# Two attentions, one gate: whole-tile stores of q and k, and row maxima on neighbouring partitions

## The chip, the cores and the metric

The kernel runs on one core of a Trainium2 chip. The metric is the device time of one execution in microseconds (us). TensorE (PE) multiplies, with its weight loads (PEld) beside it; VectorE (DVE), ScalarE (ACT) and GpSimd (POOL) do the rest; SyncE (SP) issues every transfer (DMA).

## The reference

There are 2048 positions of width 640 and 32 heads of 20. Branch A cuts the positions into four segments of 512: causal softmax attention inside a segment, plus a read from a memory matrix that earlier segments filled. Branch B is causal attention in a sliding window of 256. A gate mixes them.

```python
# A, for segment s of 4, head by head (L = 512, Dh = 20)
p = softmax(qs @ ks.T * scale + causal);  a_dot = p @ vs
a_mem = (phi(qs) @ M) / (phi(qs) @ z + 1e-6)          # phi(t) = t + 1 if t > 0 else exp(t)
o = g_h * a_mem + (1 - g_h) * a_dot
M += phi(ks).T @ vs;  z += phi(ks).sum(0)
a = concat(o) @ wo
# B, all 2048 positions
p = softmax(where(0 <= i - j < 256, q @ k.T * scale, -1e9));  b = (p @ v) @ wo_b
g = sigmoid((x * gate_w).sum(-1));  out = g * a + (1 - g) * b
```

## The kernel before

**The work.** `T` counts 16 pieces: four segments times four head groups (g = 0 and 1 are the halves of branch A's heads, 2 and 3 those of B). A piece projects q and k in five tiles of 128 rows by 512 positions (`gemm2`, L578), in split precision: x and the weights are each a rounded half and a residual (`split_h` L516, `split_l` L532), and three products make one. It projects v (`v_mm`, L730), and then has four units `u` (64 in all) of four heads each.

**Stacks.** A projected tile is itself split into a rounded half and a residual, `ml` (`m_high` on ACT, L599; `m_low` on DVE, L603), and stored to an image in DRAM (`qk_store`, L633 and L635: one of the two writes half and residual, the other the half once more). `stack_read` (L804, L807, L809) loads from it a stack `qks` of 128 partitions: two halves of 64, for two heads each, with 60 rows of q and the matching rows of k. One matmul over 60 rows thus gives a product of two split numbers. Before, a tile's rows ran over the borders of the image's blocks of 160 rows, so that a tile was stored in one or two pieces of 32 to 128 rows (`runs_of`), each with two transfers.

**Maxima.** `max_mm` (L833) computes all logits once, `max_red` (L843, DVE) takes each query's maximum; the 16 columns of maxima are split into half and residual (`max_high`, `max_low`), turned (`max_turn`), stored to DRAM (`max_store`, L859) and loaded back as two more rows of q in each half of the stack, partitions 60 and 61 and 124 and 125, by two transfers (`max_rows`, L863). The rows of k there hold -1 (`init_pad`, L485), so that the score matmul over 62 rows (`st_mm`, L887) subtracts the maximum. ACT takes the exponential (`st_exp`, L894), POOL cuts the triangle (`select`, L900 and L903), TensorE multiplies with v in four column groups (`av_mm`, L919).

**Memory.** phi(q) and phi(k) (L640 to L648) are stored by `phi_store` (L657); `mem_load` (L927) brings phi(k) into `pks`, `mem_query` (L933) phi(q) into `qfs`; `mem_add` (L966) and `mem_read` (L946) use them. `o_store` (L1035) keeps the results for the last product (`gemm2` again with `ohl`, and `gemm`, L570, for the last tile).

**The order** is written out by a planner in the program. Each step is added with a due time, an engine, an estimated cost, the buffers that it makes, changes and reads, and, for a transfer, its size. `order` then simulates the engines and picks, for each, the step that could start first, ties going to the smaller rank: the due time plus a shift by kind and a nudge, both from tables.

```python
rank = items[i][19] + nudge[i].get(step, 0.0)
...
most = min(some)[0] + (TP if pe else TO)
pick = min((z for z in some if z[0] <= most), key=lambda z: z[1:])
```

The matmuls on 64 rows belong to one of two half arrays, `pe0` and `pe1`, and two of them run side by side. A product that changes halves in its middle has a `join` there (L593), an empty instruction of ACT or DVE that waits for the first half. Steps on SP are issued in the order that the planner wrote, one behind the other; `ml` and `phi` have two buffers each, the stacks four, the ring `xst` of loads of x and of results four.

Of the kernel before, what the change touches and what calls it, by code (L numbers as in the profile page):

```python
# [10 lines left out]
F32 = mybir.dt.float32  # L11
# [22 lines left out]
WIN = 256  # L34
KW = WIN + L
# [82 lines left out]
class Plan:  # L118
# [56 lines left out]
    def link(self):  # L175
# [8 lines left out]
        for i, (t, _, eng, dur, fn, a, new, mod, put, get, size, pace, cols, _, bank, _, _, mark, behind, _) in enumerate(items):  # L184
# [217 lines left out]
def attention(ctx, tc, const, dram, xt, wqk, wv, wo, beta, o_dram, out):  # L402
# [79 lines left out]
    def init_pad(d, row, off):  # L482

        n = 32 * row // 128
        nc.sync.dma_start(bass.AP(tensor=d.tensor, offset=d.offset + off, ap=[[n, 128], [1, n]]), B["neg"][:, 0:n])  # L485
# [845 lines left out]
```

## Time and profile before

| | |
|---|---|
| time, median of 3 runs | 988.43 us (988.43, 983.97, 991.27) |
| profiled execution | 980.1 us, its span 978.4 us |
| TensorE clock granted | 1.000 |
| busy PE, PEld, DVE | 967.9, 812.6, 761.4 us |
| busy ACT, POOL | 651.7, 637.2 us |
| moved by DMA | 248.56 MB, mean 254 GB/s |

The profile is one execution. A line such as "L578 PE MATMUL ... x2400 | 453.5, 398 | 3.6" names a line of the program, an engine and an operation, what it writes and reads, how many there are; then the busy time of the group in us, the mean of one in ns, and the idle time of the engine just before them. Busy times of groups that run side by side overlap. The chain is the work that ended last, followed back from the end: a line there carries the share of the time in which that work was what all else waited for. In the view by stretches, each engine has its busy time in us with its number of instructions, then come the granted clock, the share of the DMA engines and GB/s. In the view of one line, DMA_DIRECT2D durations are the time that SP took to issue, as least/median/most in ns.

### The profile page before, as it was taken

Reading aid. Unit: us, or ns where it says so; the run is one execution under the profiler, and the core shown is the slowest. Engines: PE = TensorE matmul, PEld = TensorE weight load, DVE = VectorE, ACT = ScalarE, POOL = GpSimd, SP = SyncE. Lnnn points to the kernel's source line nnn. Section 1 sums busy time; section 2 is a strip of 40 time slices with the busy share of each in tenths; the row PEclk is TensorE's granted clock in tenths of the full one; section 3 lists DMA queues with packets and bytes.
Section 4 is the critical chain, followed back from the end, with each engine's and each line's share of the span. In section 5 each row is a group of like instructions: output and inputs, shape, how many; then the busy total and the mean of one; then the engine's idle time right before and its main releaser. Section 6 shows DMA issues by size and latency. Waiting matters only on the chain.

```text
span 978.4 us, 30482 instructions
## 1 busy us (share of the span) xinstructions
PE 967.9 (99%) x11295; PEld 812.6 (83%) x11295; DVE 761.4 (78%) x2626; ACT 651.7 (67%) x1432; POOL 637.2 (65%) x864
## 2 busy tenths in 40 slices
PE   8999999999999999999999999999999999999998
PEld 6997798888878888879888798888988888887776
DVE  3269789898899876988868888698767886788944
ACT  4527767877686776675876676676676676765671
POOL 5424467847666696757966479595795676956850
PEclk9999999999999999999999999999999999999999
DMA  8998989798898879699887887979867798487533
GB/s 276 306 306 267 290 277 275 252 293 265 279 260 283 277 220 308 205 314 298 260 264 242 254 280 207 311 224 333 285 230 234 222 296 270 137 268 215 180 99 103
DMA packets 158036, 248.56 MB, mean 254 GB/s; under 512 B 52032, under 2 KB 68288, under 8 KB 157888
## 3 DMA queue, kind: packets, MB, share of 16 engines
q1 hardware_dynamic: 157888, 246.62, 79.7%
q8 instruction: 89, 1.46, 0.6%
q14 instruction: 59, 0.48, 0.1%
HBM read 150.88 MB, written 95.68 MB: 252 GB/s over the span
## 4 chain that ended last, share of the span: by engine, by line
PE 92%; DVE 3%; DMA 3%; ACT 0%; issue 0%; POOL 0%; SPq 0%; DVEq 0%
PE bank L578 43%; PE bank L919 15%; PE bank L730 14%; PE bank L833 9%; PE bank L887 8%; DVE bank L843 2%; PE bank L570 2%; DMA wst<-wqk 1%; PE bank L946 1%; PE bank L966 1%; DMA wvs<-wv 1%; DMA xst<-xt 1%; DVE mx L843 0%; DVE ot L990 0%; SPq L524 0%
## 5 line engine op out<-in xcount | busy, mean ns | idle before, releaser
L894 ACT ACTIVATE P<-bank 128x512 f32<-128x512 f32 (+2 forms) x768 | 381.3, 556 | 148.2 <-PE bank L887 98.2
L578 PE MATMUL bank<-xhl,w 64*128 64x512 f32 x2400 | 453.5, 398 | 3.6 <-ACT xhl L516 2.8
L578 PEld LDWEIGHTS bank<-xhl,w 64*128 64x128 f32 x2400 | 325.4, 186 | 14.8 <-ACT xhl L516 3.7
L833 PE MATMUL bank<-qks 60*128 60x384 f32 (+3 forms) x1024 | 309.1, 334 | 1.3 <-DVE ot L990 0.8
L843 DVE CUSTOM_DVE_ANT_0 bank<-bank,mask_b 128x384 f32<-128x384 f32 (+2 forms) x512 | 259.7, 553 | 28.3 <-PE bank L833 21.1
L730 PE MATMUL bank<-wv,xhl 64*128 64x320 f32 (+1 forms) x1920 | 280.6, 313 | 0.2 <-POOL wv L532 0.2
L843 DVE CUSTOM_DVE_ANT_0 bank<-bank,mask_a 128x128 f32<-128x128 f32 (+3 forms) x512 | 239.9, 509 | 39.4 <-PE bank L833 29.2
L887 PE MATMUL bank<-qks 62*128 62x384 f32 (+3 forms) x1216 | 261.1, 301 | 0.4 <-DVE ot L990 0.2
L730 PEld LDWEIGHTS bank<-wv,xhl 64*128 64x128 f32 x1920 | 238.8, 186 | 3.2 <-issue 1.2
L578 PE MATMUL bank<-ohl,w 64*128 64x512 f32 x1050 | 226.3, 399 | 0.1
L532 POOL TENSOR_TENSOR w<-wst,w 128x640 fp32r<-128x640 f32 x112 | 174.9, 1565 | 77.9 <-ACT w L516 77.0
L900 POOL TENSOR_SCALAR_AFFINE_SELECT P<-P 128x512 f32<-128x512 f32 x256 | 161.5, 640 | 76.7 <-ACT P L894 71.6
L887 PEld LDWEIGHTS bank<-qks 62*128 62x128 f32 x1216 | 195.8, 185 | 15.3 <-issue 3.3
L833 PEld LDWEIGHTS bank<-qks 60*128 60x128 f32 x1024 | 177.5, 184 | 20.8 <-issue 6.2
L919 PE MATMUL bank<-P,vau 128*32 128x384 f32 (+3 forms) x2432 | 159.9, 407 | 0.2
L578 PEld LDWEIGHTS bank<-ohl,w 64*128 64x128 f32 x1050 | 152.9, 185 | 8.6 <-issue 3.3
L843 DVE DVE_READ_ACCUMULATOR2_ANT mx<- 128x1 f32 x1024 | 142.5, 139 | 0.0
L919 PEld LDWEIGHTS bank<-P,vau 128*32 128x32 f32 x2432 | 69.3, 110 | 78.6 <-issue 63.5
L516 ACT ACTIVATE w<-wst 128x640 fp32r<-128x640 f32 x121 | 89.4, 741 | 40.1 <-PE bank L578 15.7
L990 DVE STREAM_TRANSPOSE ot<-bank 128x512 f32<-128x512 f32 x64 | 45.8, 715 | 64.0 <-PE bank L919 61.6
L903 POOL TENSOR_SCALAR_AFFINE_SELECT P<-P 128x512 f32<-128x512 f32 x112 | 70.8, 641 | 4.5 <-ACT P L894 4.1
L532 POOL TENSOR_TENSOR wv<-wvs,wv 128x322 fp32r<-128x322 f32 x80 | 65.2, 834 | 11.8 <-ACT wv L516 11.5
(72 smaller groups left out, 758.9 us busy)
## 6 DMA issues: line engine op xcount, KB each, us to landing
qks<-dqk SPq DMA_DIRECT2D x32, 1024.0 KB
wst<-wqk SPq DMA_DIRECT2D x80, 320.0 KB
qks<-dkb SPq DMA_DIRECT2D x24, 768.0 KB
qks<-dqb SPq DMA_DIRECT2D x32, 512.0 KB
o_dram<-ot SPq DMA_DIRECT2D x64, 256.0 KB
wst<-wo SPq DMA_DIRECT2D x41, 320.0 KB
wvs<-wv SPq DMA_DIRECT2D x16, 805.0 KB
xst<-o_dram SPq DMA_DIRECT2D x35, 256.0 KB
```

The source lines that it names most:

```text
L516: nc.scalar.activation(dst, src, AF.Copy)
L532: EN[e].tensor_tensor(out=t[:, 1], in0=B.pop(src), in1=f(t[:, 0]), op=ALU.subtract)
L578: z = nc.tensor.matmul(B[key], B[wkey][64 * r:64 * r + 64, a, 128 * c:128 * c + 128], B[xkey, c][64 * r:64 * r + 64, b], start=start, stop ...
L730: z = nc.tensor.matmul(B["v", T, b][:, :n], B[("x", s), c][64 * r:64 * r + 64, a, 128 * b:128 * b + 128], B["wv", T, c][64 * r:64 * r + 64 ...
L833: nc.tensor.matmul(psum(("mx", u, p, b, r))[:, :n], fr(q), keys(u, 3 * DH, r, p, c0, n), start=True, stop=True)
L843: nc.vector.tensor_tensor_reduce(out=x, in0=x, in1=mk, scale=1.0, scalar=BIG, op0=ALU.add, op1=ALU.max, accum_out=B["M", u][:, j:j + 1])
L887: nc.tensor.matmul(B[k][:, c:c + 128 * n], keys(u, K, r, p, WIN + 128 * kb, 128), fr(q[64 * r:64 * r + K, L * p + 128 * q0:L * p + 128 * ( ...
L894: nc.scalar.activation(B["P", u, b][:, 2 * r + p, c0:c1], B["st", u, b, p, r][:, c0:c1], AF.Exp, scale=SCALE)
L900: nc.gpsimd.affine_select(out=v, in_=v, pattern=[[0, 4], [1, 128]], compare_op=ALU.is_ge, fill=0.0, base=0, channel_multiplier=-1)
L903: nc.gpsimd.affine_select(out=v, in_=v, pattern=[[0, 4], [-1, 128]], compare_op=ALU.is_gt, fill=0.0, base=0, channel_multiplier=1)
L919: nc.tensor.matmul(o[32 * j:32 * j + 32, 128 * q0:128 * (q0 + n)], v[:, VA * h:VA * h + 32], t[:, j, c:c + 128 * n], start=(b == 0 and i = ...
L990: nc.vector.transpose(t, B["o", u])
```

## The change

- **The weight columns** of q and k are laid out anew on the host, so that of a piece's five projected tiles two hold q alone (16 of the 20 columns of each head, one tile for each half of the stack), two k alone, and the middle one 64 rows of q and 64 of k.
- **Stores.** The four plain tiles go out whole, 128 rows at a time: one transfer writes the rounded half to both of its places, reading it twice, and waits for `m_high` alone; the other writes the residual. The middle tile goes out in six transfers of 64 rows. `phi_store` writes a tile in one transfer, or 64 rows of the middle one.
- **Stacks.** The image of the upper half starts at row 68 of each stack. Partitions 0 to 59 are the first half, 68 to 127 the second, 62 to 65 the four rows of maxima, and 60, 61, 66 and 67 are padding: q has zeros there and in the rows to be loaded, k has -1. One transfer a unit loads the maxima. The score matmul reads 64 rows in both halves, the maxima's matmul 60 in the lower and 64 in the upper. The columns of maxima are ordered to fit, so `max_high` and `max_low` write with a step.
- **Pads** are 8 transfers instead of 16, the zeros from `pks`.
- **Queries** of the memory come in 6 transfers instead of 8 for two units.
- **The first segment's x** is loaded into the five buffers `ys` instead of the ring `xst`.
- **The planner**: `join` is costed at 0.06 on both engines; nudges go by finer groups of steps, and their table is replaced whole.

```diff
+MAXR, R1 = 62, 68
...
+GROUPS = dict(
+    max_high='M', max_low='M', max_turn='M', max_store='N', max_rows='N', o_turn='O', den_eps='O', den_rec='O',
...
 NUDGE = dict(
-    a={22: 0.6},
-    c={12: 1, 39: 1.4, 47: 1.4, 51: -1.1, 53: 2.1, 74: 2.9},
...
+    a={49: -4.3},
+    c={30: -0.98, 35: 0.4, 74: 1.87},
...
+    def group(self, z):
+        return GROUPS.get(z[4].__name__, self.kind(z))
...
             for name in get:
+                if name[0] == "first":
+                    s = slot(name[1])
+                    deps[i].add(s["base"])
+                    s["gets"].append(i)
+                    continue
...
-        nudge = [NUDGE.get(self.kind(z), {}) for z in items]
+        nudge = [NUDGE.get(self.group(z), {}) for z in items]
...
-    def init_pad(d, row, off):
-        n = 32 * row // 128
-        nc.sync.dma_start(bass.AP(tensor=d.tensor, offset=d.offset + off, ap=[[n, 128], [1, n]]), B["neg"][:, 0:n])
+    def init_pad(d, row, off, key):
+        n = 8 * (R1 - 3 * DH) * row // 128
+        src, m = pks if key == "im" else B[key], min(n, L)
+        ap = [[n, 128], [1, n]] if n == m else [[n, 128], [m, n // m], [1, m]]
+        nc.sync.dma_start(bass.AP(tensor=d.tensor, offset=d.offset + off, ap=ap),
+                          src[:, 0:n] if n == m else src[:, 0:m].unsqueeze(1).to_broadcast([128, n // m, m]))
...
     def load(tag, pool, bufs, width, key, src):
         B[key] = (xpool.tile([128, L], F32, name=tag, tag=tag, bufs=bufs)[:, :width] if tag == "xst" else
+                  work.tile([128, L], F32, name=tag, tag=tag, bufs=bufs) if tag == "ys" else
...
-    def runs_of(m, kinds=(0, 1)):
...
+    PARTS = ((0, 0), (0, 1), None, (1, 0), (1, 1))
+    PIECES = [[(0, 128, 0), (0, 128, 1)], [(0, 128, 0), (0, 128, 1)], [(64 * w, 64, i) for i in range(3) for w in range(2)],
+              [(0, 128, 0), (0, 128, 1)], [(0, 128, 0), (0, 128, 1)]]
...
-    def qk_store(T, m, n, twice):
-        w, half, at, r, c = runs_of(m)[n]
+    def qk_store(T, m, n):
+        r, c, i = PIECES[m][n]
+        w, half = PARTS[m] or (r // 64, 0)
         d, row, off = image(T, w)
-        ml = f(B["ml", ("m", T, m)][r:r + c])
-        z = (2 - 2 * w) if twice else w
-        off += (512 * half + 8 * DH * z + at) * row
-        if twice:
-            nc.sync.dma_start(bass.AP(tensor=d.tensor, offset=off, ap=[[row, c], [1, L]]), ml[:, 0])
+        step = 8 * DH * row
+        if c == 128:
+            x = f(B["ml", ("m", T, m)])[:, i]
+            off += 8 * R1 * half * row + (2 - w) * step * i
+            if i:
+                nc.sync.dma_start(bass.AP(tensor=d.tensor, offset=off, ap=[[row, 128], [1, L]]), x)
+            else:
+                nc.sync.dma_start(bass.AP(tensor=d.tensor, offset=off, ap=[[row, 128], [(1 + w) * step, 2], [1, L]]),
+                                  bass.AP(tensor=x.tensor, offset=x.offset, ap=[list(x.ap[0]), [0, 2], [1, L]]))
         else:
-            nc.sync.dma_start(bass.AP(tensor=d.tensor, offset=off, ap=[[row, c], [8 * DH * row, 2], [1, L]]), ml)
+            x = f(B["ml", ("m", T, m)])[r:r + 64, i // 2]
+            off += 128 * row + ((0, 1 + w, 2 - w)[i]) * step
+            nc.sync.dma_start(bass.AP(tensor=d.tensor, offset=off, ap=[[row, 32], [8 * R1 * row, 2], [1, L]]), x)
...
-    def phi_store(T, m, n):
...
+    def phi_store(T, m, w):
         d = dphi[head(T)[0]]
+        off = d.offset + 2 * QB * w * L
+        if PARTS[m]:
+            nc.sync.dma_start(bass.AP(tensor=d.tensor, offset=off + PARTS[m][1] * L, ap=[[2 * L, 128], [1, L]]), B["phi", T, m])
+        else:
+            nc.sync.dma_start(bass.AP(tensor=d.tensor, offset=off + 256 * L, ap=[[L, 64], [1, L]]), B["phi", T, m][64 * w:64 * w + 64])
...
-                    add(t0 + NC * dt - 0.01, AD, (0.2, 0.08), join, k, mod=[k], off=-9)
+                    add(t0 + NC * dt - 0.01, AD, (0.06, 0.06), join, k, mod=[k], off=-9)
...
-        add(t + 1.1e-4, DVE, 0.61, m_low, k, mod=[ml], get=[k], off=EV)
+        add(t + 1.1e-4, DVE, 0.61, m_low, k, put=[ml], get=[k], off=EV)
+        for n, (r, c, i) in enumerate(PIECES[m]):
+            add(t + 3e-4, SP, 0.55, qk_store, T, m, n, put=[("dq", T)] if m or n else [],
+                new=[] if m or n else [(("dq", T % 4) if g < 2 else ("dq", T), 1, ("dq", T))],
+                get=[("first", ml) if i == 0 or c == 64 and i == 1 else ml], size=(4096 if c == 128 and i == 0 else 2048) * c, packet=2048)
...
     def max_mm(u, p, b, r):
+        K = 64 if r else 3 * DH
...
+    def mparts(u):
+        return mrs[u % 2].rearrange("p (r z j) -> p z r j", z=2, j=8)
...
-        nc.scalar.activation(mrs[u % 2][:, 0:16], B["M", u], AF.Copy)
+        nc.scalar.activation(mparts(u)[:, 0], B["M", u].rearrange("p (r j) -> p r j", j=8), AF.Copy)
...
-    def max_rows(u, r):
+    def max_rows(u):
         d = B["dmx", u]
-        nc.sync.dma_start(qks[u % NQ][64 * r + 3 * DH:64 * r + 3 * DH + 2, 0:2 * L], bass.AP(
-            tensor=d.tensor, offset=d.offset + 2 * L * r, ap=[[4 * L, 2], [1, 2 * L]]))
+        nc.sync.dma_start(qks[u % NQ][MAXR:MAXR + 4, 0:2 * L], bass.AP(tensor=d.tensor, offset=d.offset, ap=[[2 * L, 4], [1, 2 * L]]))
...
     def st_mm(u, b, p, r, i):
-        q, K = qks[u % NQ], 3 * DH + 2
+        q, K = qks[u % NQ], 64
...
-    for i, (d, row, off, k) in enumerate(pads):
-        add((-5.2, -2.5, 0, 2)[i // 4] + 0.01 * i, SP, DI, init_pad, d, row, off, get=["neg"], put=[k], size=2 ** 16 * row // L, packet=row)
+    for t, d, row, off, src, k in pads:
+        add(t, SP, DI, init_pad, d, row, off, src, get=[src], put=[k, "iz"] if src == "im" else [k], size=2 ** 17 * row // L, packet=2 * row)
...
-                plan_split(-20 + 0.02 * c, -20.01 + 0.02 * c, "xhl", xpool, NX, "xst", NXS, L, (("x", 0), c),
+                plan_split(-20 + 0.02 * c, -20.01 + 0.02 * c, "xhl", xpool, NX, "ys", NC, L, (("x", 0), c),
...
-        for r in range(2):
-            add(t + .04 + .001 * r, SP, DJ, max_rows, u, r, get=[("dmx", u)], put=[("qr", u)], size=8192, packet=4096, rings=2)
+        add(t + .04, SP, DJ, max_rows, u, get=[("dmx", u)], put=[("qr", u)], size=16384, packet=4096, rings=4)
...
-                for j in range(8 * (1 - u % 2)):
+                for j, (i, x) in enumerate(((0, 0), (1, 0), (2, 0), (3, 0), (0, 1), (1, 1)) if u % 2 == 0 else ()):
...
-                    add(u + ML + 0.001 * i, SP, 0.65, mem_load, T, g // 2, i, get=[("dphi", T, 1), "im"],
+                    add(u + ML + 0.001 * i, SP, 0.65, mem_load, T, g // 2, i, get=[("dphi", T, 1), "im", "iz"],
```

More of the change, by code (lines that the diff above doesn't have):

```diff
@@ L704, in plan_m @@
         add(t + 1e-4, ACT, 0.5, m_high, k, new=[("ml", 2, ml)], get=[k], off=EV)
-        add(t + 1.1e-4, DVE, 0.61, m_low, k, mod=[ml], get=[k], off=EV)
-        for n, z in enumerate(runs_of(m)):
-            for twice in range(2):
-                add(t + 3e-4, SP, 0.55, qk_store, T, m, n, twice, put=[("dq", T)] if m or n or twice else [],
-                    new=[] if m or n or twice else [(("dq", T % 4) if g < 2 else ("dq", T), 1, ("dq", T))],
-                    get=[ml], size=(4096, 2048)[twice] * z[4], packet=2048)
-        runs = phi_rows(T, m) if g < 2 else []
-        if runs:
-            zs = {w: min(x for x in range(NC) for y in phi_rows(T, x) if y[0] == w) for w in {z[0] for z in runs}}
-            new = [w for w in zs if zs[w] == m]
+        add(t + 1.1e-4, DVE, 0.61, m_low, k, put=[ml], get=[k], off=EV)
[3 more added lines that the diff above has]
+                get=[("first", ml) if i == 0 or c == 64 and i == 1 else ml], size=(4096 if c == 128 and i == 0 else 2048) * c, packet=2048)
+        ws = [w for w in phi_kinds(T) if not PARTS[m] or PARTS[m][0] == w] if g < 2 else []
+        if ws:
             add(t + 4e-5, ACT, 0.5, phi_neg, T, m, new=[("phi", 2, ph)], get=[k], off=EV)
@@ L717, in plan_m @@
             add(t + 6e-5, DVE, 0.61, phi_sum, T, m, get=[k], mod=[ph], off=EV)
-            for n, z in enumerate(runs):
-                w = z[0]
-                add(t + 7e-4, SP, 0.7, phi_store, T, m, n, get=[ph], size=2048 * z[4],
-                    new=[(("dphi", g, w), 1, ("dphi", T, w))] if w in new else [], put=[] if w in new else [("dphi", T, w)])
-                new = [x for x in new if x != w]
+            for w in ws:
+                add(t + 7e-4, SP, 0.6, phi_store, T, m, w, get=[ph], size=2 ** 18 if PARTS[m] else 2 ** 17,
+                    new=[(("dphi", g, w), 1, ("dphi", T, w))] if m == 2 * w else [], put=[] if m == 2 * w else [("dphi", T, w)])
     def v_mm(T, b, r, c, i, start, stop):
@@ L777, in plan_v @@
                 if n == 3 * NC - 1:
-                    add(t + n * dt / 3 + 1e-4, AD, (0.2, 0.08), join, k, mod=[k], off=-9)
+                    add(t + n * dt / 3 + 1e-4, AD, (0.06, 0.06), join, k, mod=[k], off=-9)
             plan_vout(t + 2 * NC * dt - 0.01 + j * 1e-3, T, b + j)
@@ L831, in max_mm @@
         c0, n = max_keys(u, b)
-        q = qks[u % NQ][64 * r:64 * r + 3 * DH, L * p + 128 * b:L * p + 128 * b + 128]
-        nc.tensor.matmul(psum(("mx", u, p, b, r))[:, :n], fr(q), keys(u, 3 * DH, r, p, c0, n), start=True, stop=True)
+        K = 64 if r else 3 * DH
+        q = qks[u % NQ][64 * r:64 * r + K, L * p + 128 * b:L * p + 128 * b + 128]
+        nc.tensor.matmul(psum(("mx", u, p, b, r))[:, :n], fr(q), keys(u, K, r, p, c0, n), start=True, stop=True)
     def max_red(u, p, b, r):
@@ L1126, in attention @@
     add(-14, POOL, 0.5, init_neg, new=[("ot", 2, "neg")])
[L1127 to L1130 removed]
+    pads = [(t, ds[i], row, (8 * 128 * h + 8 * 3 * DH) * row, src, ("ik", k, i)) for t, k, ds, row, h, src, i in
+            ((-5.2, 0, dqk, L, 0, "im", 0), (-5.19, 0, dqk, L, 1, "neg", 0), (-2.5, 1, dqb, L, 0, "im", 0), (-2.49, 2, dkb, S, 0, "neg", 0),
+             (-2.48, 0, dqk, L, 0, "im", 1), (-2.47, 1, dqb, L, 0, "im", 1), (0, 0, dqk, L, 1, "neg", 1), (2, 2, dkb, S, 0, "neg", 1))]
+    for t, d, row, off, src, k in pads:
+        add(t, SP, DI, init_pad, d, row, off, src, get=[src], put=[k, "iz"] if src == "im" else [k], size=2 ** 17 * row // L, packet=2 * row)
     add(-13, POOL, 2.0, c_mask, put=["mk"])
@@ L1257, in attention @@
             if s > 0:
-                for j in range(8 * (1 - u % 2)):
+                for j, (i, x) in enumerate(((0, 0), (1, 0), (2, 0), (3, 0), (0, 1), (1, 1)) if u % 2 == 0 else ()):
                     qk = ("qf", u // 2)
-                    add(u + QF + 0.001 * j, SP, DI, mem_query, T, g // 2, j % 4, j // 4, get=[("dphi", T, 0)],
-                        new=[] if j else [("qf", NF, qk)], put=[qk] if j else [], size=DH * 2048, packet=1024, rings=10, late=DS)
+                    add(u + QF + 0.001 * j, SP, DI, mem_query, T, g // 2, i, x, get=[("dphi", T, 0)],
+                        new=[] if j else [("qf", NF, qk)], put=[qk] if j else [], size=(1 + i // 2) * DH * 2048, packet=1024 * (1 + i // 2),
+                        rings=10, late=DS)
                 add(te + 0.03, DVE, 0.72, o_turn, u, 1, get=[("num", u), ("nub", u)], put=[ok])
```

92 lines of the change are left out of this document (49 added, 43 removed).

## The prediction

> **What bounds the kernel now.** I read the page's busy shares first, then the chain that ended last for the whole span and cut into stages, then TensorE's groups with their shapes kept apart, and last SyncE's own queue.
>
> ```profile
> PE 967.9 (99%) x11295; PEld 812.6 (83%) x11295; DVE 761.4 (78%) x2626; ACT 651.7 (67%) x1432; POOL 637.2 (65%) x864
> PE 92%; DVE 3%; DMA 3%; ACT 0%; issue 0%; POOL 0%; SPq 0%; DVEq 0%
> by line: PE bank L578 42.7%; PE bank L919 15.5%; PE bank L730 13.6%; PE bank L833 8.6%; PE bank L887 8.2%; DVE bank L843 2.0%; PE bank L570 1.8%; DMA wst<-wqk 1.4%; PE bank L946 1.3%; PE bank L966 0.7%; DMA wvs<-wv 0.7%; DMA xst<-xt 0.6%; D
> ```
>
> TensorE is busy 967.9 of 978.4 us and carries 92% of the chain; SyncE's queue, on which most of the change lies, carries 0%. But busy is not full: two 64-row matmuls can run side by side on the two halves of the array, and one that runs alone counts as just as busy. How full the time is comes from the instructions:
>
> ```profile
> 26.79 3.58 PE bank L578 x31
> 957.15 17.28 PE bank L570 x75
> L578 PE MATMUL bank<-xhl,w 64*128 64x512 f32 x2400 | 453.5, 398 | 3.6 <-ACT xhl L516 2.8 <-DVE xhl L532 0.5 <-DVE mx L843 0.3
> L578 PE MATMUL bank<-ohl,w 64*128 64x512 f32 x1050 | 226.3, 399 | 0.1
> L730 PE MATMUL bank<-wv,xhl 64*128 64x320 f32 x1440 | 208.0, 313 | 0.0
> L833 PE MATMUL bank<-qks 60*128 60x384 f32 x576 | 188.3, 354 | 0.3
> L887 PE MATMUL bank<-qks 62*128 62x384 f32 x384 | 122.6, 351 | 0.1
> L887 PE MATMUL bank<-qks 62*128 62x256 f32 x352 | 80.3, 287 | 0.0
> L887 PE MATMUL bank<-qks 62*128 62x128 f32 x352 | 72.9, 219 | 0.0
> L730 PE MATMUL bank<-wv,xhl 64*128 64x322 f32 x480 | 72.7, 312 | 0.2 <-POOL wv L532 0.2
> L833 PE MATMUL bank<-qks 60*128 60x512 f32 x128 | 49.6, 412 | 0.0
> L833 PE MATMUL bank<-qks 60*128 60x256 f32 x160 | 45.1, 296 | 0.0
> L887 PE MATMUL bank<-qks 62*128 62x512 f32 x128 | 44.5, 420 | 0.4 <-DVE ot L990 0.2
> L833 PE MATMUL bank<-qks 60*128 60x128 f32 x160 | 36.7, 240 | 1.0 <-DVE ot L990 0.8 <-DVE mx L843 0.2
> ```
>
> On the chain, 31 paired matmuls of 512 columns took 3.58 us, 0.1155 us each (75 whole-array ones took 17.28, 0.230 each, which is the same rate): 0.226 ns a column when both halves work. At that rate L578's 3450 need 398 us; L730's 615,360 columns 139; L833's 348,160 columns (576x384 + 128x512 + 160x256 + 160x128) 79; L887's, by the same count of columns, 79; L570 17; and L919, L946 and L966, at their 17.5% of the chain, 171. Together 883 us of the 978.4: **95 us are lost** to matmuls without a partner, to turns between the kinds, and at both ends. A change that leaves TensorE's instructions as they are can only win from these 95. Their place shows in the chain by stage, here 0 to 60, 60 to 240, 240 to 900 and 900 to 979 us:
>
> ```profile
> by line: PE bank L578 48.8%; PE bank L730 21.4%; DMA wvs<-wv 11.2%; DMA xst<-xt 10.1%; SPq L524 3.3%; POOL wv L532 1.5%; PE bank L833 1.0%; ACT wv L516 0.8%; issue 0.8%
> by line: PE bank L578 35.7%; PE bank L730 14.4%; PE bank L919 13.5%; PE bank L887 9.8%; PE bank L833 9.3%; DVE bank L843 5.7%; DMA wst<-wqk 3.3%; DVE mx L843 1.2%; PE bank L966 1.0%; POOL w L532 0.9%; issue 0.8%; DVE ot L990 0.7%; ACT phi L
> by line: PE bank L578 45.6%; PE bank L919 17.2%; PE bank L730 14.3%; PE bank L833 9.8%; PE bank L887 8.8%; PE bank L946 2.0%; DMA wst<-wqk 1.2%; PE bank L966 0.8%; ACT w L516 0.1%; DVE ot L990 0.1%; DVE bank L843 0.1%; ACT P L894 0.1%; issu
> by line: PE bank L578 30.3%; PE bank L570 21.9%; PE bank L919 16.9%; DVE bank L843 10.6%; PE bank L887 5.9%; PE bank L833 2.5%; DVE mx L843 1.8%; issue 1.5%; DVE ot L990 0.9%; DVE ot L993 0.9%; DVE ys L1070 0.9%; DVE ot L1030 0.7%; DVE den
> ```
>
> Up to 60 us two loads and what they release are on the chain (wvs 11.2% and xst 10.1%, 12.8 us). From 60 to 240 the terms shown off TensorE (DVE 7.6%, wst 3.3%, POOL 0.9%, issue 0.8%) make 12.6%, 23 us; from 240 to 900 TensorE's own lines add up to 98.5%, which leaves 1.5%, 10 us in eleven times 60. At the end it is DVE's row maxima again. So two thirds of the run has next to nothing to give.
>
> **The change part by part.** *TensorE's instructions*: the same count. The maxima of the upper half read 64 rows for 60, the scores 64 for 62. Rows cost nothing here: with 512 columns the rows above have 412 ns at 60, 420 at 62, 398 and 399 at 64. 0 us.
>
> *SyncE's queue*:
>
> ```profile
> L633 SPq DMA_DIRECT2D dqk<-ml x64: 308/516/2123, 23.8 to 814.5; - x64
> L635 SPq DMA_DIRECT2D dqk<-ml x64: 312/520/1736, 19.6 to 814.0; - x64
> L657 SPq DMA_DIRECT2D dphi<-phi x48: 527/684/1219, 39.4 to 793.9; - x48
> L863 SPq DMA_DIRECT2D qks<-dmx x128: 233/257/2676, 73.5 to 936.9; - x128
> L933 SPq DMA_DIRECT2D qfs<-dphi x96: 273/335/2375, 253.3 to 891.1; - x96
> L485 SPq DMA_DIRECT2D dqk<-ot x8: 319/430/550, 4.4 to 16.6; - x8
> ```
>
> A head group and segment (16 of them) stores q and k with 14 transfers instead of 16: 32 fewer at about 0.518, 16.6 us. Stores of phi go from 48 to 36 (8.2 us at 0.684), rows of maxima from 128 to 64 (16.4 at 0.257), queries from 96 to 72 (8.0 at 0.335), pads from 16 to 8 (3.4 at 0.430). That is 140 transfers and 53 us of issue, the bytes being the same. Directly it is worth 0, since no SPq line but L524 at the start is on the chain above; through what stands behind it in the queue it is worth something only where a load was late: wst at 3.3% of 180 us and 1.2% of 660, 14 us. TensorE had other work in most of that, as its idle there says:
>
> ```profile
> 0.00:20.00 20.00, 15.73 (x111) 10.81 (x113) 7.45 (x12) 10.05 (x19) 9.18 (x23) 1.00 0.86 271
> 60.00:120.00 60.00, 59.19 (x704) 49.84 (x701) 54.04 (x205) 40.29 (x94) 27.68 (x40) 1.00 0.90 276
> 180.00:240.00 60.00, 59.06 (x694) 48.76 (x692) 51.90 (x197) 47.13 (x111) 37.21 (x52) 1.00 0.86 275
> ```
>
> 0.94 us idle in the stretch with the late wst. Between nothing and 14 I take 2, near the idle rows. DVE, with 54.04 of 60 us from 60 to 120, is not relieved: its 512 x 2 reductions stay. So late next, where a load comes earlier, is DVE, with 5.7% of that stage.
>
> One joined load of maxima for two is counted above by its issue alone, 0.257 us, since the two loads stood one behind the other and no row gives a landing by itself. The Trainium skill (DMA: Bandwidth & Descriptors, "Latency and other measured facts") speaks against counting more: a tiny transfer has a shortest round trip, which it gives as about 800 ns, whatever its size, so that joining two saves no latency. By that rule the sum stays as it is; by full saving of a round trip in each of 64 units it would be up to 51 us more, all of it off the chain, and no run here shows it.
>
> *The start.* All five chunks of x now get buffers of their own (the ring had four):
>
> ```profile
> 4.37 3.30 SPq L485 DMA_DIRECT2D dqk<-ot  x4
> 8.12 0.33 SPq L524 DMA_DIRECT2D xst<-xt  x1
> 12.52 0.50 PE L578 MATMUL bank<-xhl,w 64*128 64x512 f32 x2 [1.62 <-ACT xhl L516]
> 9.08 6.70 DMA wvs<-wv
> ```
>
> The fifth load is issued at 8.12, behind four pads that take 3.30 us, and TensorE idles 1.62 us for it at 12.52. Issued with the other four, at about 3, it comes before it is wanted: 1.6 us. The two pads left in that place give wvs, issued at 9.08, at most half of 3.30, 1.65 us; but the transfers share engines that are 0.86 busy, so what x gains wvs may lose. I take 2 us, between 0 and 3.3.
>
> *What waits anew.* The first store of a tile waits for the rounded half alone and not for the residual (one DVE operation, 0.68 us, earlier). Both halves' scores now wait for one row load; SP issued the second 0.26 us after the first, so nothing is lost. The loads into pks also wait for the pads that read its zeros; those pads are issued in the first 20 us or so and the first such load at 59. The new maxima layout makes three small operations strided; 64 units times a few ns. Together 0.
>
> *The order.* The list of nudges is replaced whole, so every engine's order changes outside the arithmetic above. No row prices it. Its bounds: the 23 us of the stage from 60 to 240 falling to the 1.5% of the next one, minus 20; and a loss of the size that the same program shows between its runs, 983.97 to 991.27, plus 7. I take minus 1, close to nothing, as two thirds of the run is nearly full.
>
> Sum: 2 + 2 + 1 = 5 us less. The profiled execution took 980.1 us, 1.7 beyond its span, and goes to 975; the median of the runs shown is 8.3 above it, and from 988.4 the forecast is **983 us**.
>
> **The rivals.** *Faster: the freed queue reaches TensorE.* The Trainium skill (Perfetto Trace Analysis, "Identifying the Most-Contended Engine") judges TensorE's headroom by the weight loads' share, not by matmul time. By that, 83% here, there would be more room than the idle shows; the 95 us found above agree. The mechanism in this kernel: between 60 and 240 us stacks, rows and weights come earlier, scores and products find partners, and the 12.6% off TensorE fall by half, 11 us, with 2 to 3 from the start: 988.4 - 14 = 974. For it speaks that SP stands in a row there, against it that DVE and not a transfer leads that stage's waits.
>
> *No change: the start's gain is taken back.* The DMA engines are 0.86 busy in the first 20 us; an earlier fifth chunk delays wvs, on whose landing the first v products hang, and later stages hold no wait that SP ends. 988, give or take 3.
>
> *Slower: ScalarE held by the stores.* The middle tile of five holds 64 rows of q and 64 of k and now goes out in six transfers where it had four; two buffers of ml are all there are, and the rounding copy in ScalarE's order waits until they have landed:
>
> ```profile
>   DMA dqb<-ml: 7.5, 1
>   DMA dqk<-ml: 2.7, 2
> ```
>
> Behind it on ScalarE stand the exponentials (L894), which free the score banks. Two more issues of 0.52 in each of 16 groups are 16.6 us; were all of it to reach TensorE, less 2 at the start, 1003; it decides once these waits exceed some 25 us where they are 10 to 12 now. Against it: the other four tiles go out in two transfers each, and earlier.
>
> That the change doesn't do what it says can be left out: the counts of transfers follow from the loops.
>
> **How the numbers follow.** About 1% (10 us) is what a measurement of this kernel can tell from no change. Forecast, 978.5 to 986: 0.36. No change, 986 to 992: 0.20. Faster, 963 to 978.5 with 974 in its middle: 0.29. Slower, 992 to 1006: 0.15, of which 0.06 is still within 1%. So faster by over 1% has 0.29, within 1% 0.62, slower by over 1% 0.09. The range of 8 in 10 takes in the bounds of the start and the queue and leaves out the far ends of the two outer cases, about 0.1 each: 968 to 998.
>
> **What would show it.** Right: SyncE's counts as above; the fifth xst issued before 5 us and no idle of 1.6 us at 12; TensorE's busy time 960 to 965 with the same counts; the chain from 240 us still over 97% TensorE. Wrong: waits of the ml copies on their own stores over 25 us (the slower rival); the non-TensorE share from 60 to 240 under 7% (the faster one); or from 240 us on a share off TensorE of 4% and more, which would mean that the new order, and no transfer, sets the time.

## The result, and the profile after

The changed kernel takes **975.38 us** (median of 6 runs, 974.45 to 977.93) against 987.22 for the kernel before (6 runs, 983.77 to 991.27): ratio 0.9885, 95% interval 0.9855 to 0.9915, or 11.8 us less. Measured again, the same pair gave 0.9925 (0.9897 to 0.9952). That lies in the range of the rival "faster" and below the forecast's own 978.5 to 986.

The two profiled executions, of 980.1 and 976.76 us, are only 3.4 us apart by their spans (978.4 and 975.0). The one of before stood at the fast end of its kernel's runs, the one of after inside its narrow band. The page of after, its busy line and the engines of the chain:

```profile
PE 965.6 (99%) x11295; PEld 809.5 (83%) x11295; DVE 765.7 (79%) x2624; ACT 649.9 (67%) x1435; POOL 636.3 (65%) x863
PE 88%; DMA 5%; POOL 3%; DVE 2%; issue 1%; ACT 1%; SPq 0%; POOLq 0%; DVEq 0%; ACTq 0%
```

TensorE does as many instructions in 2.3 us less, and SyncE's queue is still at 0% of the chain. The chain by stage, 0 to 60, 60 to 240 and 240 to 900 us:

```profile
by line: PE bank L605 42.1%; PE bank L754 23.9%; DMA wst<-wqk 10.4%; DMA wvs<-wv 10.3%; SPq L551 4.2%; SPq L510 2.6%; PE bank L858 2.1%; POOL wv L559 1.5%; issue 1.0%; ACT wv L542 0.8%
by line: PE bank L605 41.8%; PE bank L754 18.3%; PE bank L947 17.1%; PE bank L858 10.8%; PE bank L915 10.4%; PE bank L998 1.3%; ACT P L922 0.3%; issue 0.0%
by line: PE bank L605 40.6%; PE bank L947 15.3%; PE bank L754 13.7%; PE bank L858 8.8%; PE bank L915 7.7%; PE bank L978 2.0%; DMA wst<-wqk 1.7%; issue 1.5%; DMA dphi<-phi 1.4%; DMA qks<-dmx 1.0%; POOL w L559 0.9%; PE bank L998 0.8%; DMA wvs
```

(The lines moved: L605 was L578, L754 was L730, L858 was L833, L868 was L843, L915 was L887, L922 was L894, L947 was L919.) From 60 to 240 us what is off TensorE fell from 12.6% to 0.3%. From 240 to 900 it rose from 1.5% to 6.5% in the terms shown alone; TensorE's own lines there add up to 88.9%, where they were 98.5%. The stretches say what this is worth in TensorE's time:

```profile
0.00:20.00 20.00, 17.98 (x127) 13.79 (x128) 7.72 (x14) 10.24 (x19) 5.75 (x20) 1.00 0.88 289
60.00:120.00 60.00, 60.00 (x722) 50.09 (x720) 52.96 (x206) 40.83 (x95) 30.11 (x41) 1.00 0.90 288
180.00:240.00 60.00, 60.00 (x714) 50.24 (x712) 53.79 (x208) 45.80 (x109) 40.19 (x53) 1.00 0.89 289
```

In the first 20 us TensorE is busy 17.98 us where it was 15.73; in the two others its idle of 0.81 and 0.94 us is gone, and 18 to 20 more matmuls fit in. The start, in the timeline:

```profile
1.25 2.31 SPq L551 DMA_DIRECT2D ys<-xt  x5
11.39 7.10 PE L605 MATMUL bank<-xhl,w 64*128 64x512 f32 x60 [0.19 <-ACTq L620]
11.52 0.46 SPq L576 DMA_DIRECT2D wvs<-wv  x1
```

The fifth load of x is issued by 3.6 us, and the idle of 1.62 us at 12.5 us is gone. The load of wvs is issued later than before, at 11.52 for 9.08: seven pads now stand ahead of it in the queue, where four did.

### The profile page after: what moved, and what is told of

The parts are those of the page before. It is cut to its first block, busy times and chain, and to the rows that moved or that the text cites. A ratio compares the mean times of both kernels' runs of the same rounds, so it can differ in the third digit from the quotient of the medians.

```text
span 975.0 us, 30300 instructions
## 1 busy us (share of the span) xinstructions
PE 965.6 (99%) x11295; PEld 809.5 (83%) x11295; DVE 765.7 (79%) x2624; ACT 649.9 (67%) x1435; POOL 636.3 (65%) x863
## 4 chain that ended last, share of the span: by engine, by line
PE 88%; DMA 5%; POOL 3%; DVE 2%; issue 1%; ACT 1%; SPq 0%; POOLq 0%; DVEq 0%; ACTq 0%
PE bank L605 40%; PE bank L947 14%; PE bank L754 14%; PE bank L858 8%; PE bank L915 8%; DMA wst<-wqk 2%; PE bank L597 1%; PE bank L978 1%; DMA wvs<-wv 1%; DMA dphi<-phi 1%; PE bank L998 1%; POOL P L931 1%; DMA qks<-dmx 1%; POOL w L559 1%; POOL P L928 1%
## 5 line engine op out<-in xcount | busy, mean ns | idle before, releaser
L922 ACT ACTIVATE P<-bank 128x512 f32<-128x512 f32 (+2 forms) x768 | 382.2, 556 | 135.9 <-PE bank L915 89.2
L605 PE MATMUL bank<-xhl,w 64*128 64x512 f32 x2400 | 450.1, 397 | 0.7 <-DVE xhl L559 0.4
L605 PEld LDWEIGHTS bank<-xhl,w 64*128 64x128 f32 x2400 | 326.4, 185 | 11.3 <-DVE xhl L559 1.5
L858 PE MATMUL bank<-qks 60*128 60x384 f32 (+7 forms) x1024 | 301.9, 331 | 1.0 <-ACT P L922 0.8
L868 DVE CUSTOM_DVE_ANT_0 bank<-bank,mask_b 128x384 f32<-128x384 f32 (+2 forms) x512 | 260.6, 554 | 32.7 <-PE bank L858 23.8
L754 PE MATMUL bank<-wv,xhl 64*128 64x320 f32 (+1 forms) x1920 | 272.4, 312 | 0.5 <-POOL wv L559 0.5
L868 DVE CUSTOM_DVE_ANT_0 bank<-bank,mask_a 128x512 f32<-128x512 f32 (+3 forms) x512 | 239.6, 513 | 34.2 <-PE bank L858 21.3
L915 PE MATMUL bank<-qks 64*128 64x384 f32 (+3 forms) x1216 | 257.4, 303 | 2.1 <-ACT P L922 0.8
L754 PEld LDWEIGHTS bank<-wv,xhl 64*128 64x128 f32 x1920 | 231.7, 185 | 3.5 <-issue 0.8
L605 PE MATMUL bank<-ohl,w 64*128 64x512 f32 x1050 | 223.4, 399 | 0.0
L915 PEld LDWEIGHTS bank<-qks 64*128 64x128 f32 x1216 | 189.5, 184 | 23.2 <-issue 6.6
L858 PEld LDWEIGHTS bank<-qks 60*128 60x128 f32 (+1 forms) x1024 | 175.8, 184 | 16.3 <-ACT P L922 4.0
L947 PE MATMUL bank<-P,vau 128*32 128x384 f32 (+3 forms) x2432 | 159.9, 407 | 0.5 <-DVE mt L884 0.3
L605 PEld LDWEIGHTS bank<-ohl,w 64*128 64x128 f32 x1050 | 150.7, 185 | 8.5 <-issue 2.5
L868 DVE DVE_READ_ACCUMULATOR2_ANT mx<- 128x1 f32 x1024 | 144.6, 141 | 0.0
L947 PEld LDWEIGHTS bank<-P,vau 128*32 128x32 f32 x2432 | 69.8, 109 | 78.3 <-issue 62.4
```

The source lines that it names most:

```text
L605: z = nc.tensor.matmul(B[key], B[wkey][64 * r:64 * r + 64, a, 128 * c:128 * c + 128], B[xkey, c][64 * r:64 * r + 64, b], start=start, stop ...
L754: z = nc.tensor.matmul(B["v", T, b][:, :n], B[("x", s), c][64 * r:64 * r + 64, a, 128 * b:128 * b + 128], B["wv", T, c][64 * r:64 * r + 64 ...
L858: nc.tensor.matmul(psum(("mx", u, p, b, r))[:, :n], fr(q), keys(u, K, r, p, c0, n), start=True, stop=True)
L868: nc.vector.tensor_tensor_reduce(out=x, in0=x, in1=mk, scale=1.0, scalar=BIG, op0=ALU.add, op1=ALU.max, accum_out=B["M", u][:, j:j + 1])
L915: nc.tensor.matmul(B[k][:, c:c + 128 * n], keys(u, K, r, p, WIN + 128 * kb, 128), fr(q[64 * r:64 * r + K, L * p + 128 * q0:L * p + 128 * ( ...
L922: nc.scalar.activation(B["P", u, b][:, 2 * r + p, c0:c1], B["st", u, b, p, r][:, c0:c1], AF.Exp, scale=SCALE)
```

## The experiments

The question after the result: which part carries the gain? My theory was the queue's relief (140 transfers fewer), the rivals the new order and the early fifth chunk of x. Diffs are cut to their main lines: `...` and the comments stand for what is left out. Differences between kernels are of ratios to the kernel before on the same chip, times 984 to 985 us. Each ratio's interval is 0.002 to 0.003 to either side, so a difference of two is uncertain by some 3.5 us. The base is the changed kernel's ratio of 0.9925 from one chip; by its first ratio, 0.9885, every cost against it would be some 4 us higher.

**The changed kernel again**, as the base of what follows.

> The changed kernel once more, unaltered, as the yardstick of its neighbours on this chip. All theories: the ratio to the kernel before is again 0.9885 within 0.003, about 975 us where the kernel before has 987.

977.56 us (975.45 to 978.98), ratio 0.9925 (0.9897 to 0.9952). That is 0.004 above the first ratio, where I expected 0.003 at most. The gain to be explained here is 7.4 us; what makes it smaller than the first pair's 11.8 is not shown; the two intervals overlap.

**New stores in the old order.** Planner, nudges, step list and the late fifth chunk are those of before; layout and transfers are new, and a planned store that is no longer needed issues nothing.

```diff
+    def qk_store(T, m, n, twice):
+        c = calls[T, m] = calls.get((T, m), -1) + 1
+        for i in ((0,), (1,), (), ()) [c] if m != 2 else ((0, 1), (2, 3), (4,), (5,))[c]:
+            qk_piece(T, m, i)      # the new store of one piece
...
     def max_rows(u, r):
+        if r == 0:                 # one joined load; the second step is empty
```

> The kernel before with its planner, tables and order kept to the step, but the new layout and transfers: whole-tile stores, joined row loads, 140 transfers fewer, 64 rows in the score matmul. A planned store that the new layout doesn't need issues nothing. The fifth chunk of x is still loaded late. Queue theory (fewer transfers let what stands behind them come earlier): most of the 12 us comes along, 976 to 980 us. Order theory (the new order is what gains, the layout only allowed it): 985 to 988, no more than 2 us gained. Start theory (most of it is the early fifth chunk): 985 to 988 as well.

978.66 us, 0.9931 (0.9903 to 0.9958). The new order and the early fifth chunk together add nothing that can be measured to it (0.9925).

**Old counts in the new order.** The same layout, bytes and order, with the transfers cut so that there are 1042 again.

```diff
     def max_rows(u):               # two loads of two rows for one of four
+        for h in range(2):
...
     def qk_store ... residual:
+                for a, z in ((0, 32), (32, 128)) if m % 2 else ((0, 128),):
...
     # phi_store: the same cut; mem_query: a loop of two; init_pad: two of 64 partitions
```

> The changed kernel in its own order, with the transfers cut up again into as many as before: two row loads a unit, eight query loads, two more stores in each of 16 groups (32 and 96 rows), 48 stores of phi, 16 pads: 140 transfers more, the same bytes. Queue theory: 8 to 12 us slower than the changed kernel, 983 to 988. Order theory: within 2 us of it, 974 to 978. Start theory: within 2 us too.

986.95 us, 1.0026 (1.0002 to 1.005): 9.9 us over the changed kernel, as the queue theory asked, and its whole gain is lost.

**The fifth chunk late**, in the new order: its load stands behind the third pad again.

```diff
+        late = todo.pop(x)         # load of x, chunk 4
+        todo.insert(pad + 1, late) # pad: the third init_pad
```

> The changed kernel in its own order, but the load of the fifth chunk of x is issued behind the third pad, near 8 us as before, where the changed kernel issues it at 3. Forecast's term: 1.6 to 3 us slower than the changed kernel, 977 to 979. Queue and order theory ask for no more than that; start theory (most of the 12 us) 983 or more. If wvs had taken the gain back: 975, no difference.

980.17 us, 0.9949 (0.9929 to 0.9968): 2.4 us more, by times alone not clear of zero. The trace shows the delay (below).

**The old counts part by part**, in the new order: 16 pads for 8; 64 more loads of rows of maxima; 68 more stores of q, k and phi and loads of queries; and the last two together. The edits are the parts of the diff above.

> The changed kernel in its own order, with 16 pads instead of 8 (each cut in two, the same bytes), all other transfers as changed. In the run with all old counts the pads stood ahead of the load of wvs and put it from 11.3 to 16.5 us. Pads theory (of the 9.4 us that the old counts cost, the start takes 6): 980.5 to 985, 4 to 7 us over the changed kernel. Spread theory (every transfer costs about the same, 9.4 us over 140): 978, 0.5 us over it.

> The changed kernel in its own order, with two row loads a unit instead of one: 64 transfers more, the same bytes. Spread theory: 4.3 us slower than the changed kernel (64 of 140 times 9.4), 981 to 983. Issue theory (what counts is the issue time of 0.26 us, a third of the whole): 3 us. Pads theory: 0 to 2 us, 977 to 979, since the chain shows nothing of it.

> The changed kernel in its own order, with the old number of stores of q and k (32 more), of phi (12 more) and of query loads (24 more), the same bytes; pads and row loads as changed. Spread theory: 4.6 us slower than the changed kernel, 981 to 983. Issue theory (0.3 to 0.7 us each, more than half of the whole): 5 us. Pads theory: 0 to 3 us, 977 to 980.

> The changed kernel in its own order with two row loads a unit and the old number of stores and query loads together, 132 transfers more, and the new pads. Singly they cost -1 and 1.9 us over the changed kernel (ratios to the kernel before 0.9913 and 0.9944, the changed kernel 0.9925). Additive theory (each costs what it costs alone): ratio 0.992 to 0.996, 1 to 2 us over the changed kernel. Slack theory (a few late transfers are free, and the queue's slack runs out when they come together): 3 to 6 us over it, ratio 0.996 to 0.999, so that with the pads (4.3 us) it makes up the 9.4 us of all old counts.

| transfers added to the changed kernel | median us | ratio (95%) | against 0.9925 |
|---|---|---|---|
| 8 pads | 981.90 | 0.9971 (0.9953 to 0.9989) | +4.5 us |
| 64 loads of rows | 976.59 | 0.9913 (0.9890 to 0.9935) | -1.2 us |
| 68 stores and queries | 979.17 | 0.9944 (0.9924 to 0.9965) | +1.9 us |
| 132, rows, stores and queries | 979.42 | 0.9949 (0.9925 to 0.9973) | +2.4 us |
| all 140 | 986.95 | 1.0026 (1.0002 to 1.0050) | +9.9 us |

(One of the eight runs with 132 took 2355.8 us and is left out of its ratio.) Pads and stores fell in the ranges of the pads theory, the 132 in that of the additive one; the rows came out just below the 977 of theirs. By the medians eight pads cost more than 132 other transfers, but those two ratios are only 0.0022 apart, within their intervals. Clear is the comparison on one chip: with 8 pads 981.90, with 64 loads of rows 976.59. The pads and the 132 together make 6.9 of 9.9 us; whether the rest is interaction or measurement stays open, as the intervals allow both. How the pads cost it, in the stretches and the timelines, first the changed kernel run again, then that with 16 pads:

```profile
20.00:40.00 20.00, 20.00 (x206) 19.17 (x208) 4.36 (x8) 8.37 (x17) 9.13 (x8) 1.00 0.94 319
11.31 0.45 SPq L576 DMA_DIRECT2D wvs<-wv  x1
80.81 2.36 PE L947 MATMUL bank<-P,vau 128*32 128x512 f32 x32
```

```profile
20.00:40.00 20.00, 17.31 (x148) 16.48 (x150) 2.99 (x6) 8.40 (x17) 10.12 (x9) 0.83 0.94 312
16.22 0.59 SPq L578 DMA_DIRECT2D wvs<-wv  x1
86.72 2.36 PE L949 MATMUL bank<-P,vau 128*32 128x512 f32 x32
```

In the new order pads stand ahead of wvs in the queue. It is issued 4.9 us later, TensorE runs out of work from 17.7 to 22.15 us (from 20 to 40 us it is busy 17.31 us, with 148 matmuls for 206), the granted clock is 0.83 there, and the first product with v comes 5.9 us later. That is the price of pads in this order: in the old one wvs was issued at 9.08 us with 16 pads (the kernel before), and at 7.97 and 7.44 us with 16 and 8 of the new ones. With the fifth chunk late the same two things show, at the start:

```profile
0.00:20.00 20.00, 16.56 (x96) 11.58 (x98) 6.40 (x13) 7.51 (x13) 3.99 (x17) 0.91 0.89 276
83.93 2.36 PE L952 MATMUL bank<-P,vau 128*32 128x512 f32 x32
```

**The new stores in the old order, with the fifth chunk early** in a buffer of its own.

```diff
+        late = todo.pop(at[4]); todo.insert(at[3] + 1, late)   # right behind the fourth
```

> The kernel before's order with the new layout and transfers, and now the fifth chunk of x loaded right behind the fourth into a buffer of its own. If the 2.6 us that the late load cost in the changed kernel's order hold here too: 2 to 3 us under the run without it, 975 to 976.5, and then level with the changed kernel or a little under it, so that the new order itself is worth nothing or less. If the start has taken it back through wvs: 978 to 979, and the new order would be worth the 1 us or so between that and the changed kernel.

979.40 us, 0.9949 (0.9931 to 0.9968), where the late one gave 0.9931: no gain, and my number missed. The first and a late product with v, first with the late chunk, then with the early one:

```profile
90.71 2.36 PE L963 MATMUL bank<-P,vau 128*32 128x512 f32 x32
929.82 2.80 PE L963 MATMUL bank<-P,vau 128*32 128x384 f32 x48
```

```profile
88.34 2.36 PE L968 MATMUL bank<-P,vau 128*32 128x512 f32 x32
926.23 2.80 PE L968 MATMUL bank<-P,vau 128*32 128x384 f32 x48
```

In these two executions 2.4 us are won at the start and 3.6 kept at 930 us. But the first of them was the slowest of its six (979.26) and the second the fastest of its ten (975.70), so this pair doesn't stand for the medians. Two chips' ratios leave anything from a gain of 1.5 to a loss of 5 us.

**The kernel before, profiled again**, one execution more.

> The kernel before once more, for a second trace. Its first trace is of an execution of 980.1 us, at the low end of its runs (980 to 990), and lay level from start to end with a trace of the new transfers in the same order. Late-transfer theory (some executions lose several us to a stack, a row or a weight that comes late, at a different place each time): an execution of 983 or more shows one or more steps of 2 to 5 us, at places where the first trace has none. Even theory (it is slower everywhere by a little): the difference grows evenly, and there are no steps.

982.87 us, 2.8 over the first execution. The difference came in small steps at different places, the largest stretch of it 2.3 us between 830 and 923 us. In that stretch the granted clock fell to half for 3.4 us, 1.7 us of full clock, which the first trace doesn't have:

```profile
918.70:922.10 3.40, 3.40 (x18) 1.91 (x22) 3.40 (x12) 1.82 (x5) 3.40 (x6) 0.50 0.41 122
```

One execution does not settle what makes others slower.

**The new layout with the old counts in the old order**: the second experiment with the transfers cut as in the third. It differs from before in its layout alone, and from the second in its 140 transfers alone.

```diff
     def max_rows(u, r):            # both planned steps load two rows again
+        nc.sync.dma_start(qks[u % NQ][MAXR + 2 * r:MAXR + 2 * r + 2, 0:2 * L], ...)
```

> The kernel before's order to the step with the new layout, but with as many transfers as before: 16 pads, 128 row loads, 96 queries, 48 stores of phi, 256 stores of q and k. Queue theory (the number of transfers is what counts): back at the kernel before, ratio 0.997 to 1.003. Layout theory (whole-tile and neighbouring rows themselves, their addresses and the earlier end of a tile's stores, gain): the ratio 0.993 that the new transfers had in this order stays, 0.991 to 0.996.

984.55 us, 0.9999 (0.9978 to 1.0020). The layout is worth nothing that can be measured, and the 140 transfers are worth 6.7 us in the old order (0.9999 less 0.9931), clear of noise and most of the 7.4. As the order of every step is the same, the two traces can be laid side by side. A product with v at two places, first in the one with 902 transfers, then in the one with 1042:

```profile
197.58 2.36 PE L963 MATMUL bank<-P,vau 128*32 128x512 f32 x32
354.95 2.80 PE L963 MATMUL bank<-P,vau 128*32 128x384 f32 x48
```

```profile
198.16 2.36 PE L974 MATMUL bank<-P,vau 128*32 128x512 f32 x32
360.64 1.72 PE L974 MATMUL bank<-P,vau 128*32 128x384 f32 x24
```

The gap grows from 0.6 to some 5.7 us, in steps: it is 2.4 us at a product at 221 us and 3.5 at the one at 326.63 (330.12 with 1042). One step more comes between that product and the next. These are SyncE's issues of a stack and a weight there, and the stretch from product to product, 902 first:

```profile
327.24 0.37 SPq L846 DMA_DIRECT2D qks<-dkb  x1
329.44 0.38 SPq L533 DMA_DIRECT2D wst<-wqk  x1
326.63:343.00 16.37, 16.37 (x230) 14.27 (x228) 13.54 (x46) 13.88 (x31) 11.42 (x16) 1.00 0.96 303
```

```profile
332.27 0.43 SPq L857 DMA_DIRECT2D qks<-dkb  x1
333.86 0.76 SPq L534 DMA_DIRECT2D wst<-wqk  x1
333.86 8.99 DMA wst<-wqk
PE bank L884 <- DMA qks<-dkb: 1.0, 1, 1.0
ACT w L526 <- DMA wst<-wqk: 1.2, 1, 1.2
330.12:348.69 18.57, 17.02 (x230) 14.36 (x228) 13.57 (x46) 13.84 (x31) 11.89 (x16) 1.00 0.82 255
```

With 140 transfers more both loads are issued 4 to 5 us later, of which 3.5 are the lag that was there; the weight, 320 KB, then takes 8.99 us to land, and its step is 30% of the chain from 320 to 350 us. The maxima wait for the stack, ScalarE waits for the weight with the exponentials behind it. The same 230 matmuls take 2.2 us longer: TensorE idles for 1.55 and is busy for 0.65 more. Over the whole trace it is mostly idle time, first 902 (span 977.5 us), then 1042 (982.5):

```profile
PE 969.3 (99%) x11295; PEld 812.3 (83%) x11295; DVE 760.5 (78%) x2626; ACT 651.0 (67%) x1432; POOL 637.2 (65%) x864
PE 968.6 (99%) x11295; PEld 811.2 (83%) x11295; DVE 760.7 (77%) x2626; ACT 652.5 (66%) x1432; POOL 638.5 (65%) x864
```

TensorE is busy 0.7 us less with 1042 transfers, and idle for 13.9 us where it was 8.2. (Its granted clock, 0.998 for 0.996, saves the second trace an estimated 2 us of busy time, so some 1.3 us may be slower matmuls.) About half of these 5.7 us lie ahead of the first product with v, at 91 us, and the rest in steps like the one shown.

**The load of wvs first**: in the changed kernel, ahead of the third pad.

```diff
+        v = todo.pop(first wv_load)
+        todo.insert(index of the third init_pad, v)
```

> The changed kernel in its own order, with one step moved: the first load of wvs ahead of the third pad, so issued near 7.5 us where it is at 11.3. If the start is still bound by wvs: 1 to 3 us under the changed kernel, 974 to 976 where it has 977. If TensorE is full by then with the first products of q and k (it is busy without a break from 11.4 to 18.5 us): no difference, within 1 us.

975.17 us, 0.9912 (0.9889 to 0.9934). wvs is issued at 7.70 us, and the first product with v comes at 80.19, where the changed kernel has 80.81. It is the lowest median here and not clear of the changed kernel's 0.9925, so no version is shown to beat it.

## Why the prediction was right or wrong

The range held the time; the point, 983, is 7.6 us too high. The first pair's gain of 1.15% is just over the bound of 1% (I gave 0.29 to over, 0.62 to within), the second pair's 0.75% just inside. Step by step:

- **TensorE's instructions, 0: right.** Rows of the first and last groups below are the maxima's 60 and 64 and the scores' 64, with 384 columns:

```profile
L915 PE MATMUL bank<-qks 64*128 64x384 f32 x384 | 119.9, 354 | 1.4 <-ACT P L922 0.8 <-DVE ot L1022 0.6
L858 PE MATMUL bank<-qks 64*128 64x384 f32 x288 | 101.2, 352 | 0.9 <-ACT P L922 0.8
L858 PE MATMUL bank<-qks 60*128 60x384 f32 x288 | 100.5, 349 | 0.1
```

   352 and 354 ns where 60 and 62 rows had 354 and 351.
- **The count of transfers: right.** 32 + 16 + 16 stores at L655, as many at L657 and 96 at L662 are 224, 14 for each of 16; phi has 36, the maxima 64, the queries 72:

```profile
L655 SPq DMA_DIRECT2D dqk<-ml x32: 327/490/2025, 21.8 to 811.5; - x32
L657 SPq DMA_DIRECT2D dqk<-ml x32: 370/414/1044, 15.7 to 810.5; - x32
L662 SPq DMA_DIRECT2D dqk<-ml x48: 512/591/1972, 28.5 to 796.0; - x48
L685 SPq DMA_DIRECT2D dphi<-phi x24: 319/421/1783, 39.5 to 786.5; - x24
L687 SPq DMA_DIRECT2D dphi<-phi x12: 472/498/1550, 34.9 to 799.9; - x12
L892 SPq DMA_DIRECT2D qks<-dmx x64: 245/308/3979, 63.8 to 935.1; - x64
```

- **The queue's relief, "between nothing and 14 I take 2, near the idle rows": the mis-sized term.** It measured 6.7 us in the old order and 9.9 in the new. The mechanism, loads that come late behind other transfers, was named; the size was read from TensorE's idle in two stretches. Idle time was the right thing to read: in the old order it accounts for nearly all of the difference of the two traces. But the rows came from an execution of 980.1 us, where that kernel's runs go to 991, and from 60 to 900 us it idled for 2.0 us only. What other executions lose was not in it: the trace with 1042 transfers in the old order (984.7 us) idles 13.9 us in all where this one has 10.5, and that of the old counts in the new order (991.7) 20.1. In the profiled pair the difference is 3.4 us, near my sum of 5.
- **The pads and wvs: wrong in sign.** I counted 3.4 us of issue in the queue and at most 1.65 of relief for wvs, taking the pads to stand where they stood. The new order put seven of the eight ahead of wvs, which came 2.4 us later. What eight pads more cost in this order, 4.5 us, since wvs delays all that follows and the clock falls with it (last section), is therefore no gain over the kernel before. What halving them gained in the old order was not measured alone.
- **The start, 2 us: not disproved.** The early fifth chunk is worth 2.4 us in the new order (2.3 by the spans of the two traces, 976.0 and 973.7) and nothing measurable in the old. "Taken back by wvs" fits the issue of wvs 2.4 us later, but nothing clear is lost with the start as the change has it: putting wvs first gained nothing clear.
- **The new order, 1 us: about 0**, 0.9931 against 0.9925, the early fifth chunk included. The sign that I gave for it (4% and more off TensorE from 240 us on) showed, with 6.5% to 11.1%, and yet the order wasn't the cause: keeping the old order gave the same time within the noise. That sign was a bad one. (TensorE's busy time, 965.6 us, was to fall to 960 to 965 and just missed it.) A transfer on the chain says that it came last, not what it cost.
- **Slower, by ScalarE held by the stores: refuted.** What the copies of `m_high` waited for, in the view of their line (us, times), holds no transfer, where it had 7.5 and 2.7 us:

```profile
  PE bank L605: 17.7, 11
  PE bank L858: 5.0, 2
  issue: 2.4, 1
  DVE phi L675: 1.7, 3
  PE bank L754: 0.6, 1
```

- **Faster, by the freed queue: this came**, with its sign (0.3% off TensorE from 60 to 240 us, where under 7% was asked for). That the gain lies in that stage isn't shown: in the old order half of the 5 us came after 240 us. That the time landed within 1.4 us of this rival's 974 is in part luck: its 11 us were to come from this stage alone, whose share off TensorE fell by 22 us, while the profiled pair differs by 3.4. The weight loads' share, by which the Trainium skill (Perfetto Trace Analysis, "Identifying the Most-Contended Engine") would judge the headroom, is 83% before and after, so the 11.8 us don't show in it. The same skill (DMA: Bandwidth & Descriptors, "Latency and other measured facts") gives the shortest round trip of a tiny transfer; that joining two loads saves none of it was my inference from it, and 64 separate loads more, at -1.2 us, give or take 3.5, agree with that.

## What to carry to other kernels

On a queue that issues in order, a transfer costs what stands behind it: look for the few loads that others wait for, and count what is issued ahead of each. See where the profiled execution stands among its kernel's runs before its waits are added up, since a good execution shows little of what the others lose. When two traces with the same order are compared, compare from one piece of work to the next: a window of fixed times holds different work in each. And read the granted clock of every run.

## What was not expected

- **The clock differs between the orders.** The granted clock was 0.91 in the first 20 us with the fifth chunk late and 0.83 from 20 to 40 us with 16 pads, 1.00 in both stretches of the changed kernel. With 16 pads, the idle and the stretches of 2 us behind it:

```profile
22.15 0.41 PE L756 MATMUL bank<-wv,xhl 64*128 64x322 f32 x2 [4.46 <-ACT wv L544]
22.00:24.00 2.00, 1.31 (x8) 1.09 (x10) 0.00 (x0) 2.00 (x6) 1.82 (x3) 0.65 1.03 394
24.00:26.00 2.00, 2.00 (x16) 2.00 (x14) 0.00 (x0) 0.80 (x2) 2.00 (x2) 0.50 1.04 398
26.00:28.00 2.00, 2.00 (x13) 1.79 (x13) 0.00 (x0) 0.00 (x0) 2.00 (x3) 0.50 1.07 284
28.00:30.00 2.00, 2.00 (x16) 1.77 (x14) 0.00 (x0) 0.00 (x0) 1.16 (x2) 0.64 0.88 309
30.00:32.00 2.00, 2.00 (x25) 1.84 (x22) 0.00 (x0) 0.59 (x2) 0.00 (x0) 1.00 1.06 409
```

   TensorE idles 4.46 us, until 22.15, for the split of wvs; then the clock stands at half for some 7 us, which takes another 3.4 us of full clock (2 us times 0.35, 0.50, 0.50 and 0.36). The Trainium skill (TensorE: Matmul & The Clock Gate, "Part 1: The HAM clock gate") says that the array goes to half clock after an idle window of about 3.4 us and back after as long a busy one; this trace agrees on the half and on an idle time beyond that, and the return took about twice as long. Other traces differ: the clock fell to 0.50 for 3.4 us each in the first 18 us with the fifth chunk late, with 1042 transfers in the old order, with the new stores in the old order and with 64 loads of rows more, after single idles of at most 1.70, 2.67, 0.94 and 0.74 us since the first matmul. In the kernel before, the idle of 1.62 us at 12.5 us left it at 1.00, and in its second trace it fell with TensorE idle for only 0.08 of 20 us. What sets it off is not shown.

   It carries a part of the gain that I had not counted. Averaged over each kernel's runs the granted clock is 0.9992 to 0.9998 in the kernels with the new order, 8 pads and the early chunk, and 0.9959 to 0.9974 in all others, the kernel before included (0.9967 on the chip of the first experiments). An estimate of what that costs is the clock missing times the time: 3.3 us for the kernel before and 0.5 for the changed kernel there, so 2.8 of some 7.4 us; 2.9 of the 4.5 us of the eight pads; 2.0 of the 2.4 us of the late chunk; but 1.3 of the 6.7 us of the 140 transfers in the old order. By this the new order and the early chunk keep some 2 us of clock and lose most of it elsewhere, which the nearly equal times hide.
- **More transfers, more spread, with an exception.** Kernels with 902 transfers spread over 3.4 to 4.7 us in five cases (6 to 12 runs; with 10 runs once 6.6); with 1042 over 6.9 and 9.4 us (12 runs each), and the kernel before over 9.7 and 10.9 us (23 runs on each of two chips). But with 1034 (132 more, 8 pads) the seven runs left spread over 4.3 us, so the count alone doesn't make it. The clock has a share in it: in the kernel before, on the chip of the first experiments, it goes from 0.993 to 1.000 between runs, an estimated 7 us. That late loads make the rest fits the steps seen above; no run tests it.
